# Top-k attention with a Fourier-mix block: where the first loads are issued, and two pieces of work a step later

## The chip, the core and the metric

The kernel runs on one core of one Trainium2 chip. The time is the device time of one execution in microseconds (us); several runs are taken, and their median is given. A profile is one further execution, recorded instruction by instruction.

The core has five engines, each with its own instruction queue, in program order: TensorE (PE, with its weight loads shown as PEld), VectorE (DVE), ScalarE (ACT), GpSimd (POOL) and SyncE (SP). An engine that must wait for a result of another stops there, and all that is queued behind the waiting instruction on that engine stops too. In the profile SPq is SP's own queue and DMA the transfers that a queue started.

## The reference, cut

```python
# q, k, v: (8 batches, 8 heads, 576, 64)
scores = q @ k.T / 8                       # per head: 576 x 576
kth    = 32nd largest value of each row
scores = where(scores >= kth, scores, -1e9)
attn   = exp(scores - max);  attn /= (sum(attn) + 1e-9)
x      = attn @ v                          # -> (8, 576, 512), heads side by side
u  = x + real(fft over channels(fft over tokens(x)))
un = (u - mean) / sqrt(var + 1e-6)         # over the 512 channels
out = u + relu(un @ w1) @ w2               # w1 512 x 2048, w2 2048 x 512
```

All arithmetic of the kernel is in float32. The weights come as 64-bit numbers and are turned to float32 on the chip.

## The kernel before, in words

**Items and steps.** Two heads of one batch make a pair; there are 32 pairs, four to a batch. The rows of a pair are cut into nine items of 128 rows (the fifth is the joined remainders, the "tails", of both heads), so a batch has 36 items and the whole kernel 288. The main loop makes one step for each item. It is a software pipeline written out in program order; no scheduler reorders it. In step i stand, on the engines:

- PE: the scores of item i+3 (L292, and L281 for the last 64 columns), copied to SBUF by ACT (L295, L285) as `S`;
- DVE: the top-32 search of items i and i+1, four rounds of MAX8 (L309) with MATCH_REPLACE8 between them (L311) for each item, interleaved;
- POOL: the bounds `nt` (L318); ACT and POOL: the mask (L325, L326); ACT: the exponential (L332), which also sums the denominators;
- PE: the transposes `tpP` of the exponentials of item i-2 (i-1 in batch 0) at L351, copied by ACT (L353) as `PT`, and the product with v (L367).

When a chunk of a pair (five or four items) is done, `attended` copies its result and the denominators `den` on ACT (L381, L386) and puts `inverse` on a list. `inverse` is two small DVE instructions on a 128x6 or 128x4 tile: add 1e-9 (L394) and a reciprocal (L397) into `rd`. One step later `to_tokens` transposes the result on PE (`tpx`, L412), and `normalise` multiplies it by `rd` into the batch's `x` (DVE, L416 and L423). The list `late_now` is emptied on DVE at the end of a step, behind the top-k operations of that step; `late_next` is the list of the step after.

**Transforms.** When a batch's `x` is complete, the Fourier transforms follow as matrix products. The token transform is done in two halves (even and odd frequencies). For each half `fold_ops` makes sums and differences of `x` (in batch 0 and 1 on DVE: `sd`, `zw`, `fg`, L458 to L498), and `dft_tokens` multiplies them on PE (`yp`, L516). Then `dft_channels` (PE, `mp`, L572) and the sum `x + mp` with its statistics (DVE, L578 to L601) go token tile by token tile, then the inverse root (L609 to L624, a chain of small POOL operations), then the transposes `tpu` (L636) that make the input of the two big matrix products, `hp` (L655) and `cp` (L670, L695).

Work is put at a step by `at(step, where, fn)`. For batch 1 (`soon`) T0 is 75: the folds stand on DVE at the end of steps 75 and 77, `ft` gives the steps of the two halves of `dft_tokens` and `fc` the first step of the channel transforms.

**Hidden units.** The two big products of a batch are cut into some hundred units, put into `queue` when they become possible (`arrivals`), and spread over the next 36 steps: `level` works out how much a step may hold by planned costs, and `some` puts units between the fixed PE work of a step. So where fixed work moves by a step, units move too.

**Start.** SP issues all loads. `load_heads` loads one pair of q, k or v in eight DMAs: for each head and half one large part (L211, 64 KB in rows of 256 bytes) and one tail (L216, 8 KB). First come q of pair 0, the identity `ident` (which PE needs for transposes), k of pair 0, then three pieces of weights, v, and q of pair 1. `prep` transposes q and k on PE (`tpq`, `tpk`, L237), and ACT copies them to SBUF (`qT` L245, `kT` L247).

In batch 0 the same engines also convert the weights: L162 and L165 split the words on DVE, L177 to L184 convert on ACT, L192 joins on POOL.

Line numbers are those of the kernel before; in the changed one the functions stand four lines lower and the main loop five or six.

Of the kernel before, what the change touches and what calls it, by code (L numbers as in the profile page):

```python
# [18 lines left out]
P = 128  # L19
TH = 32  # L20
# [39 lines left out]
def kernel(  # L60
# [9 lines left out]
    nc = tc.nc  # L70
# [4 lines left out]
    HS = S // 2  # L75
    NC = 5
    NF = NC - 1
# [20 lines left out]
    id_d = nc.inline_tensor(id_np, name="c_id")  # L98
# [10 lines left out]
    ident = const.tile([P, P], F32, name="ident", tag="ident")  # L109
# [16 lines left out]
    late_now, late_next = [], []  # L126
# [73 lines left out]
    nat, qT_of, kT_of, v_of, PT, Ssb, Wk, M8, Nt = ({} for _ in range(9))  # L200
# [2 lines left out]

    def load_heads(dst, src, pair, tail0=0):
        b, hp = divmod(pair, NPB)
        for e in range(2):
            s2 = src[b, 2 * hp + e].rearrange("(h r) d -> h r d", h=2)
            for h in range(2):  # L210
                nc.sync.dma_start(  # L211
                    out=dst[:, 2 * h:2 * h + 2, e, :],
                    in_=s2[h, 0:2 * P, :].rearrange("(t p) d -> p t d", p=P),
                )
                r0 = tail0 + TH * h
                nc.sync.dma_start(out=dst[r0:r0 + TH, NF, e, :], in_=s2[h, 2 * P:HS, :])  # L216

    def load_nat(n, pair, dst=None):
        if pair < NPAIR:
            nat[n, pair] = nat_t if dst is None else dst  # L220
            load_heads(nat[n, pair], q if n == "q" else k, pair)

    def load_v(pair):
        if pair < NPAIR:
            v_of[pair] = v_t[pair % 2]
            load_heads(v_of[pair], v, pair, TAIL)

    def prep(n, pair, pool=ps_t, tag="tp"):

        if pair >= NPAIR:  # L230
            return 0.0
        src = nat.pop((n, pair))
        t_sb = attp.tile([P, S if n == "q" else NF * P], F32, name=f"{n}T_{pair}", tag=f"{n}T")
        for c0, c1 in ((0, NF), (NF, NC)):
            tp = pool.tile([P, 4, P], F32, name=f"tp{n}_{pair}_{c0}", tag=tag)
            for c in range(c0, c1):
                nc.tensor.transpose(  # L237
                    tp[:, c - c0, :], src[:, c, :, :].rearrange("p h d -> p (h d)"), ident
                )
            if c0 == 0:  # L240
                dst, got = t_sb[:, 0:NF * P], tp.rearrange("p a c -> p (a c)")
            else:
                dst, got = t_sb[:, NF * P:], tp[:, 0, 0:TAIL]
            if n == "q":
                nc.scalar.mul(out=dst, in_=got, mul=scale)  # L245
            elif c0 == 0:
                nc.scalar.copy(out=dst, in_=got)  # L247
            else:
                for hd in (slice(0, D), slice(D, P)):
                    nc.scalar.copy(out=kt_t[hd, hd], in_=got[hd])  # L250
        (qT_of if n == "q" else kT_of)[pair] = t_sb
        return 0.7
# [123 lines left out]
    def attended(pair, ch, late):  # L376

        o, w = o_of.pop((pair, ch)), CW[ch]
        PT.pop((pair, ch))
        xT = attp.tile([P, CW[0]], F32, name=f"xT_{pair}_{ch}", tag="xT", bufs=4)  # L380
        nc.scalar.copy(out=xT[:, 0:w], in_=o[:, 0:w])  # L381
        xT_of[pair, ch] = xT
        den = den_t[pair % 3]
        if ch == 0:
            for h in range(2):
                nc.scalar.copy(  # L386
                    out=den[TH * h:TH * (h + 1), 5:6],
                    in_=den[TAIL + TH * h:TAIL + TH * (h + 1), 4:5],
                )
        c0, n = (0, 6) if ch == 0 else (6, 4)  # L390
        rd = small.tile([P, 6], F32, name=f"rd_{pair}_{ch}", tag="rd", bufs=6)

        def inverse():
            nc.vector.tensor_scalar(  # L394
                out=rd[:, 0:n], in0=den[:, c0:c0 + n], scalar1=1e-9, scalar2=None, op0=ALU.add
            )
            nc.vector.reciprocal(out=rd[:, 0:n], in_=rd[:, 0:n])  # L397

        late.append(inverse)
        rd_of[pair, ch] = rd  # L400
# [191 lines left out]
    def add_mixed(b, t):  # L592
        rows, x = ROWS[t], x_of[b]
        us = us_of[b, t > 1 and t < 4][0:rows, CHUNKS[CHUNK_OF[t][0]].index(t), :]
        nc.gpsimd.tensor_tensor(out=x[0:rows, t, :], in0=x[0:rows, t, :], in1=us, op=ALU.add)
# [149 lines left out]
    kn0 = batp.tile([P, NC, 2, D], F32, name="kn0", tag="y")  # L745
    for t, r0 in ((nat_t, TAIL), (kn0, TAIL), (v_t[0], 0), (v_t[1], 0)):
        nc.gpsimd.memset(t[r0:r0 + TAIL, NF, :, :], 0.0)
    nc.gpsimd.memset(kt_t, 0.0)
    load_nat("q", 0)
    nc.sync.dma_start(out=ident, in_=id_d.ap())  # L750
    load_nat("k", 0, kn0)
    prep("q", 0)
    prep("k", 0)

# [3 lines left out]
    def at(step, where, fn, cost=0.0):  # L758
        plan.setdefault((step, where), []).append(fn)
        costs[step] = costs.get(step, 0.0) + cost  # L760

    def beside(free, step, where, fn, cost):

        at(step, where, (lambda: fn() and 0.0) if free else fn, 0.0 if free else cost)
# [50 lines left out]
    for b in range(B):  # L815
        end = PER_BATCH * (b + 1) - 1
        last = b == B - 1
        first, soon = b == 0, b == 1
        T0 = end + (2 if first else 4)
        if first:  # L820

            def folds(b=b):
                for par, space in ((0, "own"), (1, "hT")):
                    for op in fold_ops(b, par, nc.vector, space):
                        op()
            at(T0, "dve", folds)
            ft, fc = (T0 + 1, T0 + 1), T0 + 1
        elif soon:


            for par in range(2):
                def folds(par=par, b=b):
                    for op in fold_ops(b, par, nc.vector):
                        op()
                at(T0 + 2 * par, "dve", folds)
            ft, fc = (T0 + 1, T0 + 3), T0 + 4
        elif not last:
            for par in range(2):
                def folds(par=par, b=b, T0=T0):
                    for n, op in enumerate(fold_ops(b, par, nc.gpsimd)):  # L840
                        at(T0 + 6 * par + n, "pool", op)
                at(T0, "begin", folds)
            ft, fc = (T0 + 5, T0 + 11), T0 + 12
        else:
            def folds(b=b):
                a = fold_ops(b, 0, nc.vector)
                for op in a + fold_ops(b, 1, nc.gpsimd, "PT"):
                    op()
            at(T0, "dve", folds)
            ft, fc = (T0 + 1, T0 + 3), T0 + 4  # L850
        for par in range(2):
            beside(soon, ft[par], "pe1", lambda b=b, par=par: dft_tokens(b, par), 4.3)
        for n, t in enumerate((0, 1, 4, 2, 3)):
            quick = first or soon or last
            s = fc + (0 if first else n // 3 if last else n // 2)
            beside(soon, s, "pe2", lambda b=b, t=t, q=quick: dft_channels(b, t, q), 1.75)
            if not quick:
                at(s, "pool2", lambda b=b, t=t: add_mixed(b, t))
                at(s + 1, "dve", lambda b=b, t=t: stats(b, t))
            beside(  # L860
                soon, s + (1 if quick else 2), "pe", lambda b=b, t=t: channels_first(b, t), 0.6
            )
            if first and t == 4:
                at(s + 1, "pe", lambda: (queue.extend(held), held.clear()) and 0.0)
        at(s + 1, "begin" if quick else "dve", lambda b=b: rsqrt(b))
        arrivals.append(s + (1 if quick else 2))
        at(arrivals[-1], "units", lambda b=b: (queue if b else held).extend(mlp_units(b)))

    queue, held, pending, written, now, out_next = [], [], [], set(), [0], []
# [44 lines left out]
    while i < N + 4 or plan or queue:  # L914
# [10 lines left out]
        e = items[j][2] if j < N else None  # L925
# [10 lines left out]
        if pending and pending[0][0] <= i:  # L936
            _, pp, pc = pending[0]
# [12 lines left out]
        if short:  # L950
            fixed += tok
            pair, r = divmod(i - 1, PER_PAIR)
# [28 lines left out]
            got += some(max(room * (n + 1) / len(fixed) - got, 1.1 if fn in preps else 0.0))  # L981
        if short:
            if piece is not None and r in (4, 8) and i < PER_BATCH:
                out_next.append(lambda pc=(pair, r // 8): attended(*pc, late_now))
                pending.append((i + 1, pair, r // 8))
        elif PER_BATCH <= i - 3 < N:
            pair, r = divmod(i - 3, PER_PAIR)
            if r in (4, 8):
                cost += attend(pair, r // 8)
                attended(pair, r // 8, late_next)  # L990
                pending.append((i + 1, pair, r // 8))
# [61 lines left out]
```

## Time and profile before

| what | value |
|---|---|
| median of five runs | 2030.51 us (2029.91 to 2031.68) |
| profiled execution | 2030.42 us |
| its span, first to last instruction | 2028.5 us |
| PE busy | 1891.3 us (93%), 8642 instructions |
| DVE busy | 1648.3 us (81%), 3421 |
| ACT busy | 1222.8 us (60%), 3051 |
| POOL busy | 823.4 us (41%), 1098 |
| MAX8, all forms (L309) | 1152 instructions, some 0.75 us each |
| MATCH_REPLACE8 (L311) | 864 instructions, 0.74 us each |

All times in profile lines are us from the span's start. A line of the timeline has the start, the length, the engine, the line of the code, the operation, "out<-in" by the names of the tiles with their sizes, how many in a row (x4), and, in square brackets, how long the engine stood idle before it and which instruction it was waiting for. Busy shares are means over the span; the kernel's stages have different limits, so a share alone does not tell what sets the time.

### The profile page before, as it was taken

Reading aid. Unit: us, or ns where it says so; the run is one execution under the profiler, and the core shown is the slowest. Engines: PE = TensorE matmul, PEld = TensorE weight load, DVE = VectorE, ACT = ScalarE, POOL = GpSimd, SP = SyncE. Lnnn points to the kernel's source line nnn. Section 1 sums busy time; section 2 is a strip of 40 time slices with the busy share of each in tenths; the row PEclk is TensorE's granted clock in tenths of the full one; section 3 lists DMA queues with packets and bytes.
Section 4 is the critical chain, followed back from the end, with each engine's and each line's share of the span. In section 5 each row is a group of like instructions: output and inputs, shape, how many; then the busy total and the mean of one; then the engine's idle time right before and its main releaser. Section 6 shows DMA issues by size and latency. Waiting matters only on the chain.

```text
span 2028.5 us, 27672 instructions
## 1 busy us (share of the span) xinstructions
PE 1891.3 (93%) x8642; PEld 1144.0 (56%) x8642; DVE 1648.3 (81%) x3421; ACT 1222.8 (60%) x3051; POOL 823.4 (41%) x1098
## 2 busy tenths in 40 slices
PE   5766689999999999999999999999999999998999
PEld 2433356555564655647565566647565656556655
DVE  6999899999999999889889888888889888753000
ACT  6877737676466776656666666656675666541111
POOL 4879823333133365224543364224632454223100
PEclk8576779999999999999999999999999999999999
DMA  3322200010101100001000101000000001000000
GB/s 121 101 80 94 61 7 18 24 26 19 28 16 26 26 24 24 13 24 26 23 17 14 30 19 29 18 24 21 23 24 17 23 17 35 1 13 1 11 14 11
DMA packets 133586, 57.83 MB, mean 29 GB/s; under 512 B 124352, under 2 KB 124480, under 8 KB 133440
## 3 DMA queue, kind: packets, MB, share of 16 engines
q1 hardware_dynamic: 133440, 56.06, 10.2%
q8 instruction: 70, 1.15, 0.2%
q14 instruction: 76, 0.62, 0.1%
HBM read 46.57 MB, written 9.44 MB: 28 GB/s over the span
## 4 chain that ended last, share of the span: by engine, by line
PE 79%; DVE 11%; ACT 4%; issue 3%; POOL 3%; SPq 0%; DMA 0%; POOLq 0%; DVEq 0%; ACTq 0%
PE hp L655 24%; PE cp L670 20%; PE o L367 8%; PE sp L292 7%; PE tpP L351 7%; DVE m L309 4%; DVE wk L311 3%; PE yp L516 3%; PE cp L695 3%; PE mp L572 2%; PE sp_t L281 2%; POOL wk L326 1%; PE cm L797 1%; PE tpk L237 1%; ACT wk L332 1%
## 5 line engine op out<-in xcount | busy, mean ns | idle before, releaser
L326 POOL TENSOR_TENSOR wk<-S,wk 128x576 f32<-128x576 f32 x288 | 408.1, 1417 | 878.5 <-ACT wk L325 805.1
L309 DVE MAX8 m<-wk 128x8 f32<-128x576 f32 x864 | 623.1, 749 | 5.6
L655 PE MATMUL hp<-unT,w 128*128 128x256 f32 (+1 forms) x2048 | 539.0, 410 | 2.2 <-POOL t L621 2.2
L670 PE MATMUL cp<-w,hT 128*128 128x512 f32 x1024 | 478.7, 599 | 0.0
L655 PEld LDWEIGHTS hp<-unT,w 128*128 128x128 f32 x2048 | 374.0, 191 | 127.7 <-issue 33.9
L311 DVE MATCH_REPLACE8 wk<-m,wk 128x576 f32<-128x576 f32 x576 | 427.6, 742 | 0.0
L353 ACT COPY PT<-tpP 128x512 f32<-128x512 f32 (+3 forms) x640 | 221.3, 407 | 129.0 <-PE tpP L351 126.4
L670 PEld LDWEIGHTS cp<-w,hT 128*128 128x128 f32 x1024 | 179.1, 190 | 188.3 <-issue 187.3
L351 PE MATMUL tpP<-ident,wk 128*128 128x128 f32 x1440 | 221.1, 287 | 51.7 <-ACT wk L332 50.1
L332 ACT ACTIVATE wk<-wk,nt 128x576 f32<-128x576 f32 x288 | 226.2, 785 | 61.7 <-POOL wk L326 60.5
L351 PEld LDWEIGHTS tpP<-ident,wk 128*128 128x128 f32 x1440 | 175.3, 147 | 153.0 <-ACT wk L332 73.4
L309 DVE MAX8 m<-S 128x8 f32<-128x576 f32 x288 | 214.1, 743 | 30.8 <-ACT S L285 30.3
L325 ACT ACTIVATE wk<-S,nt 128x576 f32<-128x576 f32 x288 | 227.4, 790 | 11.5 <-POOL nt L318 9.8
L659 ACT ACTIVATE hT<-hp 128x320 f32<-128x320 f32 (+1 forms) x256 | 104.6, 409 | 201.5 <-PE hp L655 200.6
L295 ACT COPY S<-sp 128x512 f32<-128x512 f32 (+1 forms) x320 | 173.8, 586 | 72.6 <-PE sp L292 71.4
L311 DVE MATCH_REPLACE8 wk<-m,S 128x576 f32<-128x576 f32 x288 | 213.6, 742 | 0.0
L367 PE MATMUL o<-PT,v 128*64 128x256 f32 (+3 forms) x1440 | 195.2, 414 | 13.2 <-ACT PT L353 11.0
L292 PE MATMUL sp<-kT,qT 64*128 64x512 f32 (+1 forms) x640 | 195.9, 685 | 0.0
L367 PEld LDWEIGHTS o<-PT,v 128*64 128x64 f32 x1440 | 111.5, 153 | 85.1 <-ACT PT L353 15.9
L192 POOL TENSOR_TENSOR w<-w,space 128x512 f32<-128x512 f32 x96 | 123.5, 1287 | 6.8 <-ACT space L183 4.3
L678 DVE TENSOR_TENSOR x<-x,ct 128x512 f32<-128x512 f32 x4 | 2.8, 692 | 132.6 <-ACT ct L676 132.6
L281 PEld LDWEIGHTS sp_t<-kt,qT 128*128 128x128 f32 (+1 forms) x322 | 52.1, 189 | 66.6 <-issue 29.1
(110 smaller groups left out, 1704.1 us busy)
## 6 DMA issues: line engine op xcount, KB each, us to landing
space<-in_moe_w_ch_dram SPq DMA_DIRECT2D x32, 512.0 KB, 3.5
nat<-in_q_dram SPq DMA_DIRECT2D x128, 64.0 KB, 1.9
v<-in_v_dram SPq DMA_DIRECT2D x128, 64.0 KB, 1.9
out_dram<-x SPq DMA_DIRECT2D x32, 256.0 KB, 2.1
nat<-in_k_dram SPq DMA_DIRECT2D x124, 64.0 KB, 1.9
nat<-in_q_dram SPq DMA_DIRECT2D x128, 8.0 KB, 1.7
v<-in_v_dram SPq DMA_DIRECT2D x128, 8.0 KB, 1.7
nat<-in_k_dram SPq DMA_DIRECT2D x124, 8.0 KB, 1.7
```

What stands on the lines that cost most here:

```text
L292: nc.tensor.matmul(sp[r], lhsT=qT[hd, q_cols], rhs=kT[hd, :], start=True, stop=True)
L295: nc.scalar.copy(out=s_t[r, keys], in_=sp[r])
L309: ops.append(lambda src=src, m8=m8: nc.vector.max(out=m8, in_=src))
L311: ops.append(lambda src=src, m8=m8: nc.vector.match_replace(w, m8, src, NEG))
L325: nc.scalar.activation(out=w, in_=Ssb[i], func=AF.Relu, scale=-FAR, bias=Nt[i][:, 1:2])
L326: nc.gpsimd.tensor_tensor(out=w, in0=Ssb.pop(i), in1=w, op=ALU.subtract)
L332: nc.scalar.activation(out=w, in_=w, func=AF.Exp, bias=Nt.pop(i)[:, 0:1], accum_out=den_t[pair % 3][:, c:c + 1],)
L351: nc.tensor.transpose(tp[:, c - c0, :], p_sb[:, k0:k0 + P], ident)
L353: nc.scalar.copy(out=pt[:, he, c0:c1, col:col + w], in_=tp[:, 0:c1 - c0, o:o + w])
L367: nc.tensor.matmul(o[D * e:D * (e + 1), c0:c1], lhsT=vv[:, c, e, :], rhs=pt[:, e, c, c0:c1], start=(c == 0), stop=(c == NC - 1),)
L655: nc.tensor.matmul(hp[:, 0:w], lhsT=w1[:, dt, P * it:P * (it + 1)], rhs=unT[:, dt, 0:w], start=(dt == 0), stop=(dt == NDT - 1),)
L670: nc.tensor.matmul(cp, lhsT=hT[:, it, P * n:P * (n + 1)], rhs=w2[:, it, :], start=(it == 0), stop=(it == NIT - 1),)
```

## The change

Three parts, with no instruction of PE, DVE or POOL added or taken away.

1. Loads: `load_heads` issues the four large parts first and then the four tails, in every call. `ident` and k of pair 0 are issued by ACT, ident first; q of pair 0 and all later loads stay with SP. ACT's nine issues come ahead of its table load and its first copies in program order.
2. Batch 0: `inverse` goes on `late_next` in place of `late_now`, so that L394 and L397 stand at the end of the following step, right before the `normalise` that uses them. This concerns six chunks: both of pairs 0 to 2 and the first of pair 3.
3. Batch 1: the two halves of the token transform stand in steps 77 and 79 in place of 76 and 78, the channel transforms from step 80 in place of 79; what follows them, the arrival of batch 1's hidden units among it, moves a step with them. The folds stay at the ends of steps 75 and 77.

```diff
-    def load_heads(dst, src, pair, tail0=0):
+    def load_heads(dst, src, pair, tail0=0, queue=None):
         b, hp = divmod(pair, NPB)
-        for e in range(2):
-            s2 = src[b, 2 * hp + e].rearrange("(h r) d -> h r d", h=2)
-            for h in range(2):
-                nc.sync.dma_start(
-                    out=dst[:, 2 * h:2 * h + 2, e, :],
-                    in_=s2[h, 0:2 * P, :].rearrange("(t p) d -> p t d", p=P),
-                )
-                r0 = tail0 + TH * h
-                nc.sync.dma_start(out=dst[r0:r0 + TH, NF, e, :], in_=s2[h, 2 * P:HS, :])
-
-    def load_nat(n, pair, dst=None):
+        queue = nc.sync if queue is None else queue
+        for tails in range(2):
+            for e in range(2):
+                s2 = src[b, 2 * hp + e].rearrange("(h r) d -> h r d", h=2)
+                for h in range(2):
+                    r0 = tail0 + TH * h
+                    if tails:
+                        queue.dma_start(out=dst[r0:r0 + TH, NF, e, :], in_=s2[h, 2 * P:HS, :])
+                    else:
+                        queue.dma_start(
+                            out=dst[:, 2 * h:2 * h + 2, e, :],
+                            in_=s2[h, 0:2 * P, :].rearrange("(t p) d -> p t d", p=P),
+                        )
+
+    def load_nat(n, pair, dst=None, queue=None):
...
+    nc.scalar.dma_start(out=ident, in_=id_d.ap())
     load_nat("q", 0)
-    nc.sync.dma_start(out=ident, in_=id_d.ap())
-    load_nat("k", 0, kn0)
+    load_nat("k", 0, kn0, nc.scalar)
...
-            ft, fc = (T0 + 1, T0 + 3), T0 + 4
+            ft, fc = (T0 + 2, T0 + 4), T0 + 5
...
-                out_next.append(lambda pc=(pair, r // 8): attended(*pc, late_now))
+                out_next.append(lambda pc=(pair, r // 8): attended(*pc, late_next))
```

More of the change, by code (lines that the diff above doesn't have):

```diff
@@ L201 @@
     x_of, o_of, xT_of, rd_of = ({} for _ in range(4))
-    def load_heads(dst, src, pair, tail0=0):
+    def load_heads(dst, src, pair, tail0=0, queue=None):
         b, hp = divmod(pair, NPB)
-        for e in range(2):
-            s2 = src[b, 2 * hp + e].rearrange("(h r) d -> h r d", h=2)
-            for h in range(2):
-                nc.sync.dma_start(
-                    out=dst[:, 2 * h:2 * h + 2, e, :],
-                    in_=s2[h, 0:2 * P, :].rearrange("(t p) d -> p t d", p=P),
-                )
-                r0 = tail0 + TH * h
-                nc.sync.dma_start(out=dst[r0:r0 + TH, NF, e, :], in_=s2[h, 2 * P:HS, :])
-    def load_nat(n, pair, dst=None):
+        queue = nc.sync if queue is None else queue
[12 more added lines that the diff above has]
+    def load_nat(n, pair, dst=None, queue=None):
         if pair < NPAIR:
             nat[n, pair] = nat_t if dst is None else dst
-            load_heads(nat[n, pair], q if n == "q" else k, pair)
+            load_heads(nat[n, pair], q if n == "q" else k, pair, 0, queue)
     def load_v(pair):
```

## The prediction, made before the changed kernel ran

> **What bounds the kernel now.** I read first the page's slices of the span, to see which engine is full where.
>
> ```profile
> PE   5766689999999999999999999999999999998999
> DVE  6999899999999999889889888888889888753000
> PEclk8576779999999999999999999999999999999999
> ```
>
> A slice is 50.7 us. PE is full from the seventh slice on, but so nearly is DVE up to about the sixteenth, and an engine that waits for another can look full when filler work stands beside it. So I took the busy times of single stretches (columns: length, then busy us and instructions of PE, PEld, DVE, ACT, POOL).
>
> ```profile
> 300.00:500.00 200.00, 195.20 (x942) 117.56 (x941) 194.20 (x405) 139.12 (x356) 64.17 (x92) 1.00 0.09 22
> 540.00:813.00 273.00, 265.88 (x1305) 160.83 (x1301) 266.83 (x550) 187.57 (x479) 118.46 (x178) 1.00 0.10 24
> 830.00:1030.00 200.00, 199.24 (x939) 119.63 (x938) 173.00 (x356) 128.69 (x329) 86.31 (x113) 1.00 0.09 23
> ```
>
> After 830 us PE is busy 199.24 of 200 and DVE 173: PE sets the time. Before it both are at 97%. Which of them leads there is told by who waits: from the timelines, the scores of items 1 to 124 that I followed lie ready in SBUF 4 to 40 us before DVE begins on them, and DVE's longest idle times between 300 and 813 us are 2.01, 0.97, 0.49, 0.43 and 0.38 us. PE's are longer, and end with a result that began on DVE:
>
> ```profile
> 507.14 3.33 PE L516 MATMUL yp<-fs,fg 128*128 128x145 f32 x16 [3.56 <-DVE fg L458]
> 523.89 0.76 PE L516 MATMUL yp<-fs,fg 128*128 128x145 f32 x4 [2.40 <-DVE fg L458]
> 525.43 3.12 PE L516 MATMUL yp<-fs,fg 128*128 128x145 f32 x12 [0.78 <-DVE fg L458]
> 813.69 1.33 PE L351 MATMUL tpP<-ident,wk 128*128 128x128 f32 x5 [3.88 <-ACT wk L332]
> ```
>
> The wait at 813.69 comes from a chain of DVE (gi, 806.8), sixteen small POOL operations (to 811.3), the mask on POOL and the exponential on ACT (812.77). So DVE sets the time from 15.3 to about 813 us, then PE. What DVE gains before 813 moves the end as long as PE can come sooner; what PE alone gains there is taken back at a later wait for DVE. The end is the time of item 126's transposes (813.69) plus a fixed amount of PE work.
>
> **Loads and queues.** The chain of waits from the start (start, us, what):
>
> ```profile
> 8.05 1.92 DMA kn<-in_k_dram
> 10.11 0.66 PE tpk L237 x2
> 11.44 2.13 PE sp L292 x4
> 14.28 0.78 PE sp_t L281 x2
> 15.33 0.77 DVE m L309
> ```
>
> DVE's 15.33 hangs on the last large k load. It is late because SP issues one load after the other:
>
> ```profile
> 0.74 0.44 SPq L211 DMA_DIRECT2D nat<-in_q_dram  x1
> 4.65 0.42 SPq L750 DMA_DIRECT2D ident<-c_id  x1
> 8.05 0.42 SPq L211 DMA_DIRECT2D kn<-in_k_dram  x1
> ```
>
> These are 16 issues in 7.31 us, 0.49 each (0.42 to 0.47 busy). In 2 to 10 us the DMA engines are 35% busy at 79 GB/s, against 95% and 305 GB/s in 10 to 16: the issue is the limit, not the transfer. The change puts nine issues (ident, 4 large k, 4 tails) on ACT and sends the tails last. No trace row shows a load issued by ACT, so its price is bounded by SP's: 0.42 as the least, and upward to several times it, since ACT has other work. I take 0.49, its nearest row. Then ACT issues ident at 0.74 and k at 1.2, 1.7 and 2.2. In the changed order the fourth k load waits until ident has landed (issue to landing 2.05 in the row of 4.65, so 2.8) and the four tails for one large k load each; the last issue ends about 5.6. ACT's table load (1.28 us, at 0.73 before, hidden then) stands behind all nine, 5.6 to 6.9, then come the two qT copies (0.71), 6.9 to 7.6. q's last large load is issued by SP at 2.2 in place of 3.67. PE's tpq is ready early; tpk follows the k loads and the qT copies free its buffers, 7.6 to 8.6; kT copy 0.59, scores from about 9.25 in place of 11.44. **Gain 2.2 us**, carried by DVE to 813. Nothing else of ACT is due before 7.9. With c for one issue on ACT, scores begin at about 9c + 4.8 (9.2 at 0.49), even with before at c = 0.74; so the bounds are a gain of 2.9 (c = 0.42) and a loss that grows by 9 us for each 1 us of c (rival C). What waits behind a slow issue is the table load and the qT copies, for them PE's tpk and scores, and for those DVE. The page's other loads (128 large and 128 small of each of q, v, 124 of k) only change order on SP, and the page's chain of the last end has SPq and DMA at 0%: nothing, hidden by pairs being loaded ahead of use; uncovered, one tail's 1.7 us.
>
> The Trainium skill ("DMA: Bandwidth & Descriptors", section "Issuing engines are not separate DMA queues") speaks against this: two issuing engines share the same 16 DMA engines, and save only the issue time, usually small beside the transfer. By that the 2.2 would be about nothing, and the sum below 3.6 (2026.8). The 0.49 us an issue at 35% DMA use goes the other way here.
>
> **Inverses.** Of each head pair in batch 0, the two instructions L394 and L397 go from the end of the step in which ACT copies `den` to just before the next step's normalise. Six pairs of instructions move, none is added. What they cost now:
>
> ```profile
> 61.72 0.17 DVE L394 TENSOR_SCALAR rd<-den 128x6 f32<-128x6 f32 x1 [1.18 <-ACT den L386]
> 120.07 0.17 DVE L394 TENSOR_SCALAR rd<-den 128x6 f32<-128x6 f32 x1 [0.86 <-ACT den L386]
> 183.06 1.03 DVE L394 TENSOR_SCALAR rd<-den 128x6 f32<-128x6 f32 x1 [3.44 <-ACT den L386]
> 248.84 0.17 DVE L394 TENSOR_SCALAR rd<-den 128x6 f32<-128x6 f32 x1 [3.73 <-ACT den L386]
> ```
>
> Together 9.21 us of waits, but not all on the path. At 61.72 DVE is the chain before and after: 1.18, less about 0.5 for the new place at 68, where POOL's L192 is at work (the instruction takes 0.77 to 1.03 where it ends with a POOL operation, 0.17 where POOL is idle). Net 0.7. At 120.07 (first wait of a stretch in which ACT, PE and POOL carry the chain) nothing. At 183.06 POOL is full (three L192 of 1.29, a mask of 1.41 and other work, 6.6 us a step): DVE waits for the weights' conversion at 197.74 against 197.5 by that route, so 0.25. At 248.84 the next bound is the last normalise of the batch: item 35's exponential ends at 263.6, its transposes 263.76, tpx ends 269.1, while DVE comes there at 270.20; so 1.05 of the 3.73 is gained, the fold starts at 269.6 in place of 270.65, and tpx is late next. **Gain 0.7 + 0.25 + 1.05 = 2.0 us**; bounds: 9.2 (all waits) and a loss of 1 (a longer hold behind POOL at each new place).
>
> **Batch 1's transforms a step later.** Nothing is added; the token transforms come behind steps 77 and 79 instead of 76 and 78, the channel transforms, their sums and statistics at 80 and on. PE gets the 6.6 us of other work that followed, before yp0, so its 3.56 goes. The second half has yp1 reached at about 520.5, while DVE's second fold gives fg only at 523.89: about 3 to 4 us of the wait stay. This alone gives the end nothing, since DVE is the bound: PE is just further ahead, and 813.69 waits longer for ACT. What does count are DVE's waits for PE here: 0.16 (538.79) and 0.43 (548.75) for mp, which comes before its new place, and 0.97 (574.26) for tpx, which PE reaches sooner. 0.49 at 650 is behind two other PE waits and I leave it. **Gain 1.6 us**; bounds: 6.7, if PE's 6.74 were the path, and a loss of 1, if the statistics' move holds item 80's masks. The hand-over of the folds' buffer has room: yp0 would end at 513.3, and the second fold first writes it at 519.17, 5.9 later. The planner moves hidden units by a step (32 back units ahead of item 74's transposes where 34 stood) and is even again by item 104.
>
> **Sum:** 2.2 + 2.0 + 1.6 = 5.8. The profiled execution took 2030.42 (span 2028.5 and 1.9 outside it), so 2024.6; the median of the runs is 2030.51, so 2024.7.
>
> **Rivals.** (A) The PE idle at batch 1 is gained in full: 2.2 + 2.0 + 6.7 = 10.9, 2019.6. For: PE is at 97%. Against: the scores' lead and the 3.88 at 813.69. Chance 0.10. (B) The waits only move, as DVE after an early finish waits for the same conversions and POOL: the 2.2 or the 2.0, not both, and little of the last: 1 to 3.9, about 2028. For: the chain between 107 and 248 is mixed. Chance 0.27. (C) Slower: ACT's nine issues, ahead of its table load, cost much more than SP's. With 2.0 + 1.6 gained elsewhere, it decides against the change from a loss of 3.6 on (c = 1.1); for a loss beyond 0.2% it takes 7.7 us (c = 1.6), which gives about 2035. Against: a load's 0.42 to 0.47 on SP. Chance 0.12, with what the moved hidden units may upset. My forecast has 0.51.
>
> **How the numbers follow.** 0.2% is 4.06 us, about what a measurement can tell from no change, so the bar is 2026.4. The forecast, with its own range of 2022 to 2027.5, lies mostly beyond it; with A and the share of the forecast that falls short (0.04 of 0.51) faster has 0.57, same 0.31, slower 0.12. The range takes in half of A and most of B and C's beginning: 2019 to 2031.
>
> **What would show it.** Right: DVE's first MAX8 at about 13.1 instead of 15.33, ACT's table load at 5 to 6, no wait for den at 61.72 and 248.84, the first fold of batch 0 about 4 to 5 us sooner than 270.65, PE's 3.56 at 507 gone with some 3 left at the second half, the wait at 813.69 longer than 3.88 and its time 5.8 sooner. Wrong: a first MAX8 after 15, DVE idle in new places in 60 to 270, 813.69 moved by less than 4, or new PE waits after 830, where each counts in full.

## The result, and the profile after

The changed kernel took 2034.45 us (median of 23 runs, 2029.66 to 2036.21), the kernel before 2030.31 us (41 runs): slower by 4.1 us, ratio 1.002 (1.0015 to 1.0026). Forecast were 2024.7 and 5.8 us faster. The profiled execution has a span of 2031.8 us, 3.3 longer.

The start went much as foretold. From the chain of waits of the changed kernel (start, us, what):

```profile
1.74 3.01 DMA kn<-in_k_dram
4.78 1.32 DMA kn<-in_k_dram
6.10 1.27 ACT L249
9.82 2.13 PE sp L296 x4
13.70 0.77 DVE m L313
```

DVE begins at 13.70 instead of 15.33. Its waits for `den` in batch 0 are all gone; where 1.18 and 3.73 us stood before, the timeline has no idle time in brackets:

```profile
64.97 0.16 DVE L398 TENSOR_SCALAR rd<-den 128x6 f32<-128x6 f32 x1
246.55 0.16 DVE L398 TENSOR_SCALAR rd<-den 128x6 f32<-128x6 f32 x1
```

The first fold starts at 266.04 instead of 270.65, 4.6 us sooner. By the start of DVE's first MAX8 of an item, the changed kernel is 4.0 us ahead of the kernel before at item 60 (407 us), 1.7 at item 75, 3.9 at item 84 and 1.0 at item 100 (650 us), and 2.8 us behind at item 126 (795 us). These are PE's waits in that time (timeline, idle time and releaser in brackets):

```profile
505.39 2.39 PE L520 MATMUL yp<-fs,fg 128*128 128x145 f32 x16 [1.25 <-DVE fg L462]
512.45 1.33 PE L355 MATMUL tpP<-ident,wk 128*128 128x128 f32 x5 [2.56 <-ACT kT L251]
523.23 2.02 PE L520 MATMUL yp<-fs,fg 128*128 128x145 f32 x13 [1.54 <-DVE fg L462]
564.33 4.54 PE L371 MATMUL o<-PT,v 128*64 128x256 f32 x20 [3.29 <-DVE x L427]
816.47 1.33 PE L355 MATMUL tpP<-ident,wk 128*128 128x128 f32 x5 [3.89 <-ACT wk L336]
```

The waits for `fg` fell from 6.74 us to 2.79, as meant. But PE now stands 2.56 us at 512 and 3.29 us at 564, where the product with v needs the buffer that DVE's `normalise` has not read yet. The 20 matmuls after it take 4.54 us; before they came without a wait and took 2.38:

```profile
569.05 2.38 PE L367 MATMUL o<-PT,v 128*64 128x256 f32 x20
```

The granted clock shows why (third number from the right in the busy times by stretch, here of the changed kernel):

```profile
510.00:520.00 10.00, 7.55 (x19) 3.58 (x20) 9.84 (x17) 6.66 (x19) 3.19 (x4) 0.66 0.08 29
560.00:570.00 10.00, 6.71 (x31) 4.10 (x30) 9.32 (x23) 2.80 (x9) 3.76 (x14) 0.66 0.00 0
```

In both slices PE had 0.66 of its clock. That is 3.4 us of 10, most of it on top of the wait. And then it is DVE that waits, for PE:

```profile
572.26 0.43 DVE L420 TENSOR_TENSOR x<-tpx,rd 128x256 f32<-128x256 f32 x1 [2.83 <-PE tpx L416]
600.16 0.42 DVE L420 TENSOR_TENSOR x<-tpx,rd 128x256 f32<-128x256 f32 x1 [1.88 <-PE tpx L416]
622.90 0.42 DVE L420 TENSOR_TENSOR x<-tpx,rd 128x256 f32<-128x256 f32 x1 [1.63 <-PE tpx L416]
```

Before, DVE's waits for PE from 538 to 651 us came to 2.05 us. The stretch in which both were at 97% before now has DVE at 95%, and within it PE has no room at all:

```profile
540.00:813.00 273.00, 264.92 (x1280) 160.80 (x1278) 260.10 (x540) 184.07 (x470) 114.21 (x171) 0.99 0.10 24
640.00:790.00 150.00, 149.89 (x732) 88.81 (x731) 145.33 (x293) 105.30 (x273) 73.91 (x101) 1.00 0.11 27
```
Item 126's transposes come at 816.47, 2.8 us later than before instead of 5.8 sooner.

**A measure for the rest.** PE has the same matmuls to do in every kernel, so what it loses between 480 and 830 us can be compared: its idle time in the timeline plus, for each slice of 10 us, 10 times the clock that was missing. This is bookkeeping, not a cause, but it finds the place.

| kernel | idle 480–640 | clock loss | idle 640–830 | clock loss | sum | time less that of before |
|---|---|---|---|---|---|---|
| before | 8.8 | 3.4 | 5.8 | 3.4 | 21.4 | 0 |
| loads and inverses (e12) | 8.3 | 5.1 | 5.5 | 3.4 | 22.3 | -2.3 |
| changed | 12.9 | 6.8 | 5.5 | 3.4 | 28.6 | +4.1 |
| f4, one tpx in pool mm | 9.8 | 3.4 | 5.5 | 3.4 | 22.1 | -1.9 |
| g1b, both rates back | 12.3 | 5.1 | 2.6 | 0.0 | 20.0 | -4.1 |
| h1, first rate back | 12.2 | 5.1 | 5.6 | 3.4 | 26.3 | +0.7 |
| h2, second rate back | 12.8 | 6.8 | 2.6 | 0.0 | 22.2 | -1.1 |
| h4, both rates and tpx | 9.1 | 3.4 | 2.6 | 1.7 | 16.8 | -7.5 |
| i1, e12 with a lower rate | 8.6 | 5.1 | 3.7 | 0.0 | 17.4 | -6.8 |

Times are medians against the runs of before in the same comparison. From the changed kernel to h4 the sum falls by 11.8 and the time by 11.6. Each row is a single profiled execution, and a low clock inside a wait is counted twice, 0.7 to 1.8 us a row. The sum does not always follow the time: f1 (23.6) and f2 (23.8), which are not in the table, lie above e12 in the sum and not above it in the time, and e3, with 25.5, is slower (+3.2) than h1 with 26.3.

### The profile page after: what moved, and what is told of

Same layout as the page of the kernel before. It is cut to its first block, busy times and chain, and to the rows that moved or that the text cites. A ratio compares the mean times of both kernels' runs of the same rounds, so it can differ in the third digit from the quotient of the medians.

```text
span 2031.8 us, 27728 instructions
## 1 busy us (share of the span) xinstructions
PE 1888.9 (93%) x8642; PEld 1143.9 (56%) x8642; DVE 1647.7 (81%) x3421; ACT 1222.0 (60%) x3051; POOL 821.4 (40%) x1098
## 4 chain that ended last, share of the span: by engine, by line
PE 76%; DVE 13%; ACT 4%; POOL 4%; issue 3%; DMA 0%; ACTq 0%; POOLq 0%; DVEq 0%
PE hp L659 23%; PE cp L674 20%; PE o L371 7%; PE sp L296 6%; PE tpP L355 6%; DVE m L313 5%; DVE wk L315 4%; PE cp L699 3%; PE yp L520 3%; PE mp L576 2%; PE sp_t L285 2%; POOL wk L330 1%; PE cm L802 1%; PE tpx L416 1%; PE tpk L241 1%
## 5 line engine op out<-in xcount | busy, mean ns | idle before, releaser
L322 POOL TENSOR_TENSOR nt<-m,cc 128x2 f32<-128x2 f32 x288 | 55.6, 193 | 114.5 <-DVE m L313 113.0
## 6 DMA issues: line engine op xcount, KB each, us to landing
space<-in_moe_w_ch_dram SPq DMA_DIRECT2D x32, 512.0 KB, 3.6
```

## The experiments

**Which part.** Each part alone, and the first two together.

e1, the loads alone: the changed kernel without the edits of parts 2 and 3.

> Only the loads of the change (two queues, tails last). Theory T1: the slowing is the transforms' step alone, and what DVE gains before batch 1 reaches the end. Then the 1.63 us by which DVE's first MAX8 comes sooner in the changed kernel (13.70 for 15.33) shows: 2028.7, 1.6 under before. Theory T2: DVE and PE are nearly even from 550 to 813 us, a shift of the start only changes which of them waits for the other, and the end moves in either direction: anything from 2029 to 2034.

2028.2 against 2030.12: -1.9, ratio 0.9988 (0.9979 to 0.9997). In its profile the gain of 1.5 us at DVE's first MAX8 is still 1.4 at item 126: what DVE gains at the start does reach the end.

e2, the inverses alone:

```diff
-                out_next.append(lambda pc=(pair, r // 8): attended(*pc, late_now))
+                out_next.append(lambda pc=(pair, r // 8): attended(*pc, late_next))
```

> Only batch 0's inverses a step later. T1: DVE reaches batch 0's fold some 3 us sooner (the changed kernel gained 5.7 us by item 40, of which 1.6 came from the loads), of which about 2 reach the end: 2028. T2: as for the loads, 2029 to 2034, with PE waits between 480 and 570 us other than before.

2029.38: -0.7, ratio 0.9995 (0.9987 to 1.0004), not clear of nothing. DVE is 3.0 us ahead at item 36 and 1.1 at item 44, as a new wait takes half of it:

```profile
317.48 0.76 DVE L309 MAX8 m<-S 128x8 f32<-128x576 f32 x1 [1.54 <-ACT S L285]
```

e3, the transforms alone:

```diff
-            ft, fc = (T0 + 1, T0 + 3), T0 + 4
+            ft, fc = (T0 + 2, T0 + 4), T0 + 5
```

> Only batch 1's transforms a step later. T1: this is the harm: PE's waits at L516 shrink, but a wait of about 3 us for DVE's normalise turns up at the product with v some 40 us later, with a granted clock near 0.66 for 10 us, and DVE then waits for PE at tpx: 4 to 8 us over before, 2035 to 2038. T2: the step alone does little, 2029 to 2032; it hurts only with DVE and PE placed as the other two parts place them.

2033.33: +3.2, ratio 1.0017 (1.0009 to 1.0026). The wait at L367 is there (3.27 us), though without the low clock after it in this profile. The time lies between the ranges of the two theories, T1 (2035 to 2038) and T2 (2029 to 2032).

e12, parts 1 and 2:

> Loads and inverses, transforms as before. T1: both gains add, 2026 to 2027. T2: no such sum, 2030 to 2034, like the changed kernel.

2027.82: -2.3, ratio 0.999 (0.9981 to 0.9999). So the transforms' step is the harm, 3.2 us alone and 4.1 + 2.3 = 6.4 beside the other two. T1 named the right part; its size alone was less than T1 said. No run shows why it is larger beside the other two.

**Which half of that part.** All on top of loads and inverses. f1 has `ft, fc = (T0 + 2, T0 + 4), T0 + 4`, f2 `(T0 + 2, T0 + 3), T0 + 4`, f3 `(T0 + 1, T0 + 3), T0 + 5`. Theory A of the forecasts blames the later arrival of the hidden units, theory B the wait at L367.

> The changed kernel with both halves of the token transform a step later, but the channel transforms and the arrival of batch 1's hidden units back at the old step (fc = T0 + 4). Theory A (the later arrival costs: hidden units move from before 565 us to after it, where PE has hardly any idle time left): the loss goes, 2027 to 2029, near the 2027.8 of loads and inverses alone. Theory B (the wait of the product with v, L367, for DVE's normalise costs: PE stands 3.3 us and then has a lower clock): only if that wait shrinks too; with it still near 3 us the time stays at 2032 to 2034.

2027.8 against 2030.56: -2.8, ratio 0.9988 (0.9979 to 0.9997). No harm, as A said.

> The changed kernel with only the first half of the token transform a step later; second half, channels and arrival as before. A: no harm, 2027 to 2028.5; PE's 3.56 us at the first half is gone, and turns up as a longer wait at another place, without gain. B: the wait at L367 appears once PE runs ahead, here by the 3.56 us alone: about half the harm, 2030 to 2032.

2026.93: -3.6, ratio 0.9987 (0.9978 to 0.9996). PE's 3.56 us at the first half went, and its wait at the second grew to 7.44: no gain over e12 that could be measured.

> Loads and inverses, token transforms at the old steps, channel transforms and the arrival of hidden units a step later (fc = T0 + 5). A: this is the harmful half, 2032 to 2035. B: PE is no further ahead of DVE than before, since the waits at L516 stay: 2027 to 2029.

2031.29: +0.7, ratio 1.0005 (0.9996 to 1.0014), 3 us over e12 and between A's 2032 to 2035 and B's 2027 to 2029. Harm comes with `fc`, the channel transforms and the arrival of batch 1's units. The wait at L367 is only 0.72 us here, so it is not the whole of it. PE's wait for the first half, 3.56 us in e12, has grown instead:

```profile
504.82 3.77 PE L520 MATMUL yp<-fs,fg 128*128 128x145 f32 x16 [7.70 <-DVE fg L462]
```

DVE again waits for tpx (1.42 at 597.69, 1.59 at 620.39).

**The wait at L367.** f4 is the changed kernel with one tpx taking its buffer from another pool of buffers (`mm`), so that the product with v need not wait for it:

```diff
-                tok.append(lambda: to_tokens(pp, pc, not short))
+                tok.append(lambda: to_tokens(pp, pc, not short and (pp, pc) != (NPB * 2, 0)))
```

> The changed kernel, in which the transposes tpx of one chunk (batch 2's first pair, first chunk) take a buffer of the pool mm, so that the following product with v (L367) need not wait until DVE's normalise has read them. A: the wait of 3.3 us goes, but PE had few units to spare: it waits elsewhere, 2032 to 2034. B: 3 us of idle time and the lower clock after it go: 2028 to 2031.

2028.65: -1.9 against before, so 6 us better than the changed kernel and within B's 2028 to 2031.

g2, the same edit on e12, as a control:

> Control for the tpx buffer: loads and inverses only (transforms as before, no wait at L367 between 540 and 600 us), with the same one tpx in the pool mm. If the 5.8 us of that edit came from the wait it took away, nothing changes here: 2027 to 2028.5. If the edit is worth something by itself, 2024 to 2026.

2027.51 against 2030.19: -2.7, ratio 0.9988 (0.998 to 0.9997), like e12. The edit is worth something only where the wait is.

**The planner's rates.** `level` spreads batch 0's units from step 39 to the next arrival, which the change moves from step 82 to 83: 5.06 us of PE work a step became 5.00. Batch 1's units then have 44 steps instead of 45 up to step 127: 5.26 became 5.34. g1b sets the old rates in the changed kernel:

```diff
-            step_us = level(i)
+            step_us = {39: 5.06, 83: 5.26}.get(i) or level(i)
```

> The changed kernel with the planner's two rates for hidden work put back to those of before: 5.06 us a step from step 39 (the change makes it 5.00, as batch 0's units are spread over 44 steps instead of 43) and 5.26 from step 83 (5.34, as batch 1's have 44 steps instead of 45). Theory L (the rates: 0.08 us a step more in a stretch where PE has no idle time): most of the loss goes, 2028 to 2031. Theory W (PE stands at L367 because batch 1's units are not there yet in steps 82 and 83 and PE has run ahead): the wait of 3.3 us stays and the time with it, 2033 to 2036.

2026.14: -4.1, ratio 0.998 (0.9971 to 0.9989), 8.2 better than the changed kernel. That is 2 us under the range of theory L (the rates are the harm), although the wait that theory W blamed is still there, by PE's timeline of g1b:

```profile
563.29 3.99 PE L371 MATMUL o<-PT,v 128*64 128x256 f32 x20 [3.37 <-DVE x L427]
810.57 0.77 PE L355 MATMUL tpP<-ident,wk 128*128 128x128 f32 x5 [1.83 <-ACT wk L336]
```

and by stretches:

```profile
810.00:820.00 10.00, 9.43 (x55) 6.64 (x56) 9.74 (x24) 6.94 (x19) 3.11 (x4) 1.00 0.01 2
```

The wait at item 126 fell from 3.89 to 1.83 us, and the clock after it stayed at 1.00, where the changed kernel had 0.79 in that slice.

h1 puts back only the first rate (`{39: 5.06}`), h2 only the second (`{83: 5.26}`).

> The changed kernel with only the first rate put back (5.06 us a step from step 39, batch 0's hidden units; from step 83 the new 5.34). If the first rate carries the loss (PE, with less hidden work, runs ahead of DVE and stands at 480 to 570 us), nearly all of the 8.3 us comes back: 2026 to 2027. If the second does, only the 2.3 us by which PE's idle time and clock loss between 480 and 640 us were smaller with both rates back: 2032.

2030.34 against 2029.69: +0.7, ratio 1.0004 (0.9996 to 1.0013); 3.5 better than the changed kernel.

> The changed kernel with only the second rate put back (5.26 us a step from step 83; from step 39 the new 5.00). If the second rate carries the loss (0.08 us a step too much where PE is full, then a longer wait at item 126 and the lower clock after it): the 6.3 us by which PE lost less after 640 us with both rates back: 2028. If the first does, 2033 to 2034.

2028.64: -1.1, ratio 0.9998 (0.9989 to 1.0006); 5.2 better. Both rates cost. h1 lies between its two forecasts (2026 to 2027 and 2032), h2 near its first (2028).

h4 adds f4's edit to g1b:

> The changed kernel with both rates back and the one tpx in the pool mm, so that the wait of 3.4 us at L367 goes. If lost time of PE is lost wherever it stands: 3.4 and the clock's 1.7 less, 2021 to 2023. If DVE sets the arrival of item 126 all the same, the wait there grows by as much as the other shrinks: 2026 to 2028.

2022.23: -7.5, ratio 0.9964 (0.995 to 0.9977). Against g1b's -4.1 the wait at L367 costs some 3.4 us with the old rates too (the intervals reach 1.8 and 2.7 us to either side). The wait at item 126 stayed at 1.83, but here a stretch at half clock followed it (1.7 us lost).

i1 leaves the transforms where they were and lowers the second rate by as much: e12 with `{82: 5.18}`.

> Loads and inverses, transforms at the old steps, and batch 1's hidden units at 5.18 us a step from step 82 (5.26 before), which puts them later by about as much as in the kernel with both rates back. If the gain of that kernel is the rate's (the wait of item 126 falls from 3.9 to 1.8 and the lower clock after it goes, about 5 us), it shows without moving the transforms: 2023 to 2025. If the moved transforms are needed for it, 2027 to 2028.

2023.33 against 2030.13: -6.8, ratio 0.9965 (0.9952 to 0.9979). The rate alone gains 4.5 us over e12, and i1 is no slower than g1b, which has the transforms moved (-4.1). So nothing here shows that moving the transforms is worth anything. Item 126 in i1:

```profile
808.53 0.77 PE L355 MATMUL tpP<-ident,wk 128*128 128x128 f32 x5 [1.84 <-ACT wk L336]
```

**The loads again.** g3 is before with only the order changed (large parts, then tails, all on SP).

> The kernel before, with only the order of the loads changed: tails last, all on SP as before, no load on ACT. If the order alone does it, the last large k load is issued at about 6.6 in place of 8.05, DVE's first MAX8 comes at about 13.9 and the time is 1.4 under before: 2028.9. If the second queue is what gains, the first MAX8 stays near 15 and the time within 0.5 of before.

2029.47 against 2030.19: -0.7, ratio 0.9997 (0.9988 to 1.0005). First MAX8 at 14.72: between the two, and not measurable in the time.

g4 is f2 with the first k tails on SP, behind q's; h3 is g1b with the same edit.

> First half of the token transform alone a step later (the best so far, 2026.9), and the four k tails of the first pair issued by SP behind q's tails, so that ACT's table load does not wait for k loads to land (at 6.08 us in the changed kernel). If those waits held the start, the table load comes at 3 to 4 us, DVE's first MAX8 at 12.5 to 13.0 in place of 13.7, and the time is 0.7 to 1.2 lower: about 2026. If the k loads' landing (4.7 to 6.1 us) holds it, no change: 2026.9.

2026.56: -3.6, ratio 0.9982 (0.9973 to 0.9991). The table load moved to 3.33 and the first MAX8 to 12.74, as foretold; against f2 the median falls by only 0.4.

> The changed kernel with both rates back, and the first k tails issued by SP. With DVE's first MAX8 about 0.9 us sooner (12.74 for 13.66 in the two kernels where this was seen), 2025.3 if that reaches the end; 2026 to 2027 if PE, not DVE, now sets the time from 560 us on.

2024.41 against 2029.69: -5.3, ratio 0.9974 (0.9964 to 0.9984); 1.2 better than g1b, each against the kernel before in its own comparison; this too is within the intervals.

h5 has all that gained:

> The best parts together: the changed kernel with both rates back, the first k tails issued by SP, and the one tpx in the pool mm. If the gains of the last two (1.7 and 3.9 us) add: 2020.5. If PE sets the time after 560 us alone, the start's share is lost: 2022.

2021.58 against 2030.13: -8.6, ratio 0.9959 (0.9947 to 0.9972), the fastest version that was run, 13 us under the changed kernel. Whether the tails' edit adds to h4 stays open: 1.1 us is within the intervals.

## Why the prediction was wrong

**Start (2.2 foretold).** Right in kind, 1.63 in the profile and 1.9 in e1. An issue on ACT is busy 0.41 us, like SP's, so rival C had no ground. The sum missed that the loads land later when both queues send: k took 3.01 and 1.32 us in the chain, not 1.92, and ACT's tails, and so its table load (6.08), waited for them. The Trainium skill's rule ("DMA: Bandwidth & Descriptors", section "Issuing engines are not separate DMA queues") that only issue time is saved fits the later landings, but that time was not small here: the DMA engines' share from 2 to 10 us rose from 0.35 to 0.79, and g3, with one queue, got 0.6 of the 1.6 us.

**Inverses (2.0 foretold).** The waits went as foretold, and the fold came sooner by the foretold 4 to 5 us. The term missed what is late next after batch 0: the scores' copy, 1.54 us. What was left, 0.7 alone, is not clear of nothing. In single profiles DVE's lead at item 60 ranged from 1.5 to 3.9 us between kernels whose code is the same up to there (e12, f1, f2, g2), so one profile says little here.

**Transforms (1.6 foretold as gain; 6.4 lost).** Two steps failed. The first is "is even again by item 104": the planner's units were written down at nothing because they come out even. The profile before gave the means to see the price: PE was busy 148.34 of 149 us from 641 to 790, so there was no room for the 0.08 us more a step, 3.5 us over 44 steps:

```profile
641.00:790.00 149.00, 148.34 (x735) 88.93 (x733) 146.32 (x298) 105.77 (x274) 75.84 (x102) 1.00 0.11 27
```

That the 0.06 us less a step before step 83 let PE run ahead of DVE is argued, not shown. h1, h2 and g1b show what the rates cost: 3.5 us for the first, 5.2 for the second, 8.2 for both, each within some 2 us. DVE's first MAX8 of the items shows where, against the kernel before: from item 60 to 100 the changed kernel falls back 3.0 us, h2 (second rate back) 3.5, h1 (first rate back) 0.1; from item 100 to 120 the changed kernel and h1 fall back 3.3 us, h2, g1b and e12 nothing.

The second is "PE is just further ahead, and 813.69 waits longer for ACT". The lead was not kept until 813. PE spent it at 564, on a buffer that DVE frees, and fell back from there: 3.29 us of wait, 3.4 us of clock. The wait at item 126 was the same as before, 3.89. "DVE sets the time to 813" was too simple. Both engines were at 97%, and the rows told which one waited at each place, not which had room. Between 560 and 813 us each waits for the other in turn, and what one lost at its wait the other did not give back.

Of the rivals A and B saw no harm. C had the sign, and its chance took in "what the moved hidden units may upset"; but its price was slow issues on ACT, so it is luck that its 2035 lies near the measured 2034.45. Of the four signs that the forecast would be wrong, two came: 813.69 moved by less than 4, and the wrong way, and DVE was idle in new places in 60 to 270 (1.10 us at 249.43 and 0.66 at 260.36, for the scores' copy). A first MAX8 after 15 and new PE waits after 830 did not come.

What stays open: why the lower second rate shortens the wait at item 126. The rows show one difference. In the six kernels with that rate at 5.26 from step 83 or 5.18 from step 82 (g1b, h2 to h5, i1), one unit of four `cp` matmuls is left over and stands after 790 us, shortly before item 126's transposes, as here in g1b:

```profile
797.31 1.88 PE L674 MATMUL cp<-w,hT 128*128 128x512 f32 x4
```

There the wait is 1.8 us. In the other 14 kernels the last such unit ends by 777 us and the wait is 3.9. That PE then has work where it stood idle, and that DVE reaches item 126 sooner, both fit the lines; no run moves that unit alone.

## What to carry to other kernels

When a step is moved, ask what else is planned from its date: here a rate that fills every step changed by 0.06 to 0.08 us and was worth more than the wait that the edit took away. Where two engines are both at 97%, a wait of the one is not free because the other is the bound; look for the next buffer that one frees for the other. And test a planner's number by itself before moving work: i1, one constant, gained 4.5 us over e12, where the moved step had been forecast to gain 1.6.

## What the hardware showed

A PE wait was often followed by a stretch at half clock. In the changed kernel the granted clock is 0.50 from 512.0 to 518.8, from 563.2 to 570.0 and from 815.7 to 822.6, and each such stretch loses 3.4 us, about as much as the waits themselves (2.56, 3.29 and 3.89 us). Between 480 and 830 us every stretch at half clock in the 20 kernels' traces lost either 3.4 or 1.7 us.

Whether a wait is followed by one is not told by its length alone. The traces' clock records change only at marks 3.41 us apart: 512.0, 518.8, 563.2, 570.0 and 815.7 in the changed kernel are 2, 13, 2 and 72 times 3.413 us from one another. In other executions the marks lie elsewhere. Where PE, at full clock, was idle for 2.0 us or more between two neighbouring marks, the clock after the second was 0.50 in all 40 cases between 480 and 830 us. With 1.7 to 1.85 us idle it was so in 3 of 7, and with less in two cases in all. So the 2.56 us at 512, of which 2.1 lie between two marks, were followed by half clock. The 3.27 us at L367 in e3, cut by a mark into 1.4 and 1.8, were not. The 1.8 us at item 126 were in h4 and h5, and were not in g1b, h2, h3 and i1. Part of the clock loss in the table above is therefore where the marks happened to lie in that one execution.

The Trainium skill ("TensorE: Matmul & The Clock Gate", section "Part 1: The HAM clock gate (the "warmup" mystery)") puts the drop to half clock after an idle window of about 3.4 us that runs freely. The halving and the 3.41 us agree with these rows, but a window that was idle for 2.0 us was enough here.

The addition on `den`, a 128x4 instruction of 0.16 us elsewhere (L394 before, L398 in the changed kernel), was held for 2.33 us at 767 before and for 2.83 us at 769 in the changed kernel.
